# Transposing q and k in two row halves, loading dilated v without overlap, and reordering constants and weights in an attention and gated-unit kernel

## The chip, the cores and the metric

The kernel runs on one core of one Trainium2 chip. The metric is device time in microseconds (us); lower is better. A profiled execution gives a span, from the first to the last instruction, and a time of its own that is a little longer.

## What is computed

Two stages follow each other. The first is sliding-window attention over 8 batches and 8 heads, 576 positions, head size 64; heads 0 to 3 see the last 32 positions ("plain"), heads 4 to 7 every fourth of the last 128 ("dilated"). The second is a gated unit over the 512 joined columns.

```python
pos = np.arange(S)
rel = pos[:, None] - pos[None, :]
mask_plain = (rel >= 0) & (rel < window)
mask_dil = (rel >= 0) & (rel < window * dilation) & (rel % dilation == 0)
...
attn = np.exp(scores)
attn = attn / (np.sum(attn, axis=-1, keepdims=True) + 1e-09)
return np.matmul(attn, v).astype(np.float32)
...
for k in range(K):
    gate_pre += conv_w[k][None, None, :] * xp[:, k:k + S, :]
gate = 1.0 / (1.0 + np.exp(-gate_pre))
val = x @ w_val
return (gate * val @ w_out).astype(np.float32)
```

## The kernel before, in words

The work is cut into 16 units: for each batch one dilated and one plain unit of four heads (dilated first, except in the last batch). A unit has two halves of two heads, called `e`. For each unit q and k are loaded (576 KB each, one transfer on SP's queue), brought to bf16 (the dilated ones by reading the high half of each fp32 value, the plain ones by casts on POOL), transposed on TensorE with an identity (line 469, nine 128x128 transposes per matrix into a pair of PSUM banks), and copied to `qT` and `kT` in SBUF, each matrix in two halves on ACT or DVE (line 323 or 325). Then come scores (line 488), exp (508), masks (514), attention products (525 dilated, 552 plain), norms (535, 564) and transposes back to `xT` (573, 589).

When both units of a batch are done, the gated unit follows for each of four column groups: convolution by diagonal weights (607), tanh (615), val product (622), gate (631), and, per 128 rows, the output product (638), a copy to one of six `osb` buffers (643) and a store (652).

Three tile shapes occur on TensorE: whole array (128*128, called `F`: transposes, dilated attention products, val, outputs), two row halves (64*128, `R`: dilated scores, plain attention products) and four quarters (64*64, `Q`: plain scores, convolution).

The order on every engine is written by a planner (class `Plan`): each task has a key (a priority, in part from the table `KEY`), an assumed duration, the engines that may run it, and dependencies; a greedy list scheduler lays out the whole program and the instructions are issued in that order. [...]Where the planner expects TensorE to idle, it puts in matmuls on a zero tile (`warm`, line 666). Loads and stores share SP's queue; a load waits there until enough of the earlier ones have landed, so that few are in flight.

What the change touches:

- `load_q` (422), `load_vd` (434): loads. Dilated v is loaded in two overlapping pieces per unit: `va0` holds 80 keys, `va1` 112 more behind 16 rows of zeros (`Z1`), since the second block of 72 queries needs keys that the first piece already brought. `cv` (787) casts them to `vd0` and `vd1` on POOL.
- `transposes` (461), `evict_t` (474): the transposes of q and k and their way out of PSUM.
- `scores`, `attn_d`, `norm_d`, `transpose_xd`: the blocks of queries, `QB = 72` twice.
- the constants (`band` to `dve_consts`, 328 to 396): identities, masks and zeros, most of them on POOL, and `diag` (673), the diagonal weights, on POOL.
- `WV = 0` and `WO = 1` in `KEY`: w_val is loaded behind the loads of unit 0, w_out behind those of unit 1.

The dependencies of the transposes and of the casts:

```python
TQ[u] = add(f"T{name}{u}", j0 + KEY["T"], {"PE": (0.50, 0.67)},
            lambda t, u=u, name=name: transposes(t, u, name),
            [L[u] if d else C[u], c_eye], cfg="F", need="pair", mm=JP)
...
cvv[(u, e, z)] = add(f"cv{i}{z}", 2 * i + KEY["cv"], {"POOL": (0.57, 0.63)}, cv,
                     [ldv[u][z]] + dep, port=("POOL",))
```

Of the kernel before, what the change touches and what calls it, by code (L numbers as in the profile page):

```python
# [1 line left out]

# [11 lines left out]
def hi_bf16(ap: bass.AP) -> bass.AP:  # L14
# [5 lines left out]
KEY = {"L": 171.6, "cv": -104.8, "T": -8.3, "ET": -139.2, "S": -21.7, "X": -137.2, "M": -69.8, "A": -31.3,  # L20
       "N": -35.2, "XT": 3.1, "XE": -124.1, "C": -15.3, "H": -46.4, "V": -4.0, "G": -205.2, "O":
       33.0, "P": -86.6, "SP": 2, "W": 10.4, "WV": 0, "WO": 1}
# [19 lines left out]
class Plan:  # L42
# [50 lines left out]
    def start_of(self, t, eng):  # L93
        s = self.free_at[eng]
        if eng == "PE" and t.cfg != self.cfg and self.cfg is not None:
            s += self.SWITCH
# [132 lines left out]
def kernel(  # L229
# [10 lines left out]
    nc = tc.nc  # L240
# [8 lines left out]
    QB = TT // 2  # L249
    KB = (80, 128)  # L250
    T1 = TT - KB[1]
    Z1 = 16
# [9 lines left out]
    ETW = 400  # L262
# [25 lines left out]
    xnd = [consts.tile([QB, 8, 2, D], BF16, name=f"xnd{i}") for i in range(2)]  # L288
# [8 lines left out]
    ident_f = consts.tile([8, 8], FP32, name="ident_f")  # L297
    mask_d = consts.tile([128, HALF], BF16, name="mask_d")
# [29 lines left out]
    def band(dst, base, pattern, step):  # L328
        nc.gpsimd.affine_select(out=dst, in_=dst, compare_op=ALU.is_ge, fill=0.0,
                                base=base, pattern=pattern, channel_multiplier=-step)  # L330
        nc.gpsimd.affine_select(out=dst, in_=dst, compare_op=ALU.is_ge, fill=0.0,
                                base=W - 1 - base, pattern=[[-a, n] for a, n in pattern],
                                channel_multiplier=step)

    def eye(dst, n):
        nc.gpsimd.memset(dst, 0.0)
        nc.gpsimd.affine_select(
            out=dst, in_=dst, compare_op=ALU.not_equal, fill=1.0,
            base=0, pattern=[[-1, n]], channel_multiplier=1)

    def const(name, eng, dur, emit, deps=(), key=-50):
        return plan.add(name, key, {eng: (dur, dur + 0.05)}, lambda t: emit(), deps,
                        port=("POOL",))

    c_warm = const("warm0", "DVE", 0.5, lambda: nc.vector.memset(warm, 0.0), key=-60)  # L345
    c_eye = const("eye", "POOL", 1.0, lambda: eye(ident_b, 128), key=-60)
# [4 lines left out]
    c_sw = const("swap", "DVE", 0.25, swapped_eye, deps=[c_eye], key=5)  # L351

    def dil_mask():
        nc.gpsimd.memset(mask_d, 1.0)
        for z in range(2):
            band(mask_d[:, 2 * QB * z:2 * QB * (z + 1)].rearrange("p (h t) -> p h t", h=2),
                 z * (QB - T1), [[0, 2], [1, QB]], 1)

    c_md = const("mask_d", "POOL", 1.6, dil_mask, key=-57)

    def dil_ones():
        for x in vds[0] + vds[1] + vpb:
            nc.gpsimd.memset(x[:, :, :, D:DA], 1.0)
    c_vd = const("ones_d", "POOL", 0.4, dil_ones, key=-56)

    def small_eyes():
        eye(ident_f, 8)
        eye(ident_2[0:64], D)
        nc.gpsimd.tensor_copy(ident_2[64:128], ident_2[0:64])
    c_id = const("eyes", "POOL", 0.9, small_eyes, key=-55)  # L370

    def plain_mask():
        nc.gpsimd.memset(mask_p, 1.0)
        for s in range(2):
            m = mask_p[0:64, s, 0:96]
            nc.gpsimd.affine_select(out=m, in_=m, compare_op=ALU.is_ge, fill=0.0,
                                    base=W - s, pattern=[[1, 96]], channel_multiplier=-2)
            nc.gpsimd.affine_select(out=m, in_=m, compare_op=ALU.is_ge, fill=0.0,
                                    base=s - 1, pattern=[[-1, 96]], channel_multiplier=2)
        for g in range(1, NG):  # L380
            nc.gpsimd.tensor_copy(mask_p[0:64, :, 96 * g:96 * g + 96], mask_p[0:64, :, 0:96])
        nc.gpsimd.tensor_copy(mask_p[64:128], mask_p[0:64])
        nc.gpsimd.memset(mask_p[0:W // 2, :, 0:96], 0.0)
    c_mp = const("mask_p", "POOL", 2.6, plain_mask, key=-10)

    def dve_consts():
        for x in kTs:
            nc.vector.memset(x[:, 0:W], 0.0)
            nc.vector.memset(x[:, W + 2 * S:], 0.0)
        for x in ets:  # L390
            nc.vector.memset(x[:, :, HALF:], 1.0)
        nc.vector.memset(xT[:, :, :, 0:K - 1], 0.0)
        nc.vector.memset(vps[0][0:W // 2, 0], 0.0)
        for x in vas[1]:
            nc.vector.memset(x[0:Z1], 0.0)
    c_dv = const("dve_consts", "DVE", 2.2, dve_consts, key=-59)
# [25 lines left out]
    def load_q(u, name):  # L422
# [4 lines left out]
        if d:  # L427
            return [nc.sync.dma_start(
                out=dst, in_=src[b, hs].rearrange("h (p j) d -> (h p) (j d)", j=JD))]
# [4 lines left out]
    def load_vd(u, n, z):  # L434
        b = units[u][0]
        rows = v[b, 4:8].rearrange("h (p r) d -> p h (r d)", r=R)
        if z == 0:
            return [nc.sync.dma_start(out=vas[z][n % 2], in_=rows[0:KB[0]])]
        return [nc.sync.dma_start(out=vas[z][n % 2][Z1:KB[1]], in_=rows[T1 + Z1:TT])]

# [20 lines left out]
    def transposes(t, u, name):  # L461
        d = units[u][1]
        if d:
            src = (qns if name == "q" else kns)[u % NQ]
        else:
            src = (qcs if name == "q" else kcs)[(u // 2) % 2]
        ps = pair(t).bitcast(BF16)
        for j in range(JP):
            nc.tensor.transpose(  # L469
                out=ps[:, j * 128:(j + 1) * 128],  # L470
                in_=hi_bf16(src)[:, j * 128:(j + 1) * 128] if d else flat(src[:, j]),
                identity=ident_b)

    def evict_t(t, tr, u, name, half):
        dst = kTs[u % 2][:, W:W + 2 * S] if name == "k" else qTs[u % 2]
        pv = pair(tr).bitcast(BF16)[:, 0:JP * 128].rearrange("p (j a) -> p a j", j=JP)
        dv = dst.rearrange("p (a j) -> p a j", j=JP)
        a = slice(64 * half, 64 * half + 64)
        copy(t, dv[:, a], pv[:, a])

    def scores(t, i, hf):
# [10 lines left out]
        if units[u][1]:  # L492
            for z in range(2):
                for hh in range(2):
                    o = (2 * e + hh) * 2 * TT + hf
                    for x in range(2):
                        mm(0, 128, (2 * z + hh) * QB, QB, x, W + o + 2 * z * T1, 2,
                           o + 2 * z * QB, 2)
# [18 lines left out]
    def attn_d(t, sc, i, hf):  # L517
# [3 lines left out]
        for z in range(2):  # L521
            for x in range(2):
                for hh in range(2):
                    c = 2 * z + hh
                    nc.tensor.matmul(out=ps[:, x * 512 + c * DA:x * 512 + (c + 1) * DA],  # L525
                                     lhsT=et[0:KB[z], x, c * QB:c * QB + 128],
# [3 lines left out]
    def norm_d(t, sc, i, hf):  # L530
        av = pair(sc).rearrange("p (x c) -> p x c", x=2)[0:QB, :, 0:4 * DA].rearrange(
            "p x (n c) -> p x n c", n=4)
        rec = work.tile([QB, 2, 4], FP32, name="rec", bufs=3)
# [4 lines left out]
            in0=av[:, :, :, 0:D], in1=rec[:, :, :, None].to_broadcast([QB, 2, 4, D]),  # L538
# [29 lines left out]
    def transpose_xd(t, i):  # L568
        xn = xnd[i % 2]
        pv = bank(t).bitcast(BF16)[:, 0:S].rearrange("p (r t) -> p r t", r=R)  # L570
        for r in range(R):
            for z in range(2):
                nc.tensor.transpose(out=pv[:, r, QB * z:QB * z + QB],  # L573
                                    in_=flat(xn[:, 2 * r + z]),
                                    identity=ident_b[0:QB, 0:QB])
# [81 lines left out]
    def conv_tr(t):  # L657
# [15 lines left out]
    T_DG = add("diag", 4, {"POOL": (2.4, 2.5)}, lambda t: nc.gpsimd.tensor_tensor(  # L673
        out=diag, in0=ident_2[:, None, :].to_broadcast([128, NCH * K, D]),
        in1=conv_w[:, :, None].to_broadcast([128, NCH * K, D]), op=ALU.mult),
        [T_CE, c_id], port=("POOL",))
# [249 lines left out]
```

## Time and profile before

| what | us |
|---|---|
| median of three runs | 186.14 |
| lowest and highest run | 184.7 and 188.52 |
| the profiled execution, its own time | 189.71 |
| its span | 188.0 |
| mean granted TensorE clock | 0.984 |

The profile names an instruction by line, engine, operation, output and input. Its groups of instructions give the busy time, the mean duration of one, and the idle time of the engine just before. Some of the groups that the change touches (busy us, mean ns after the bar's left side; then idle us and what ended it):

```profile
L323 ACT COPY qT<-ps 128x576 bf16<-128x576 bf16 x26 | 15.7, 642 | 6.4 <-PE ps L469 5.6
L325 POOL CAST vd<-va 80x512 bf16<-80x512 f32 (+1 forms) x32 | 19.3, 632 | 44.8 <-DMA va<-in_v_dram 35.3
L666 PE MATMUL ps<-warm 128*128 128x512 bf16 x52 | 15.1, 415 | 2.4 <-DVE warm L345 1.3
```

The loads, with size and median us from issue to landing:

```profile
qn<-in_q_dram SPq DMA_DIRECT2D x16, 576.0 KB, 5.4
kn<-in_k_dram SPq DMA_DIRECT2D x16, 576.0 KB, 6.9
...
va<-in_v_dram SPq DMA_DIRECT2D x8, 448.0 KB, 7.8
va<-in_v_dram SPq DMA_DIRECT2D x8, 320.0 KB, 7.0
```

Matmuls overlap, so that the duration of one is not its price: the distance between the starts of two neighbours is. An engine that sits idle costs nothing unless something on the way to the end waits for it.

### The profile page before, as it was taken

How to read it: one execution, taken by the hardware profiler on the slowest of the kernel's cores; microseconds unless marked ns; L12 is line 12 of the kernel's file. 1: busy time of each engine (PE TensorE's matmuls, PEld its weight loads, DVE VectorE, ACT ScalarE, POOL GpSimd, SP SyncE). 2: the span in 40 equal slices, each digit the busy share in tenths (PEclk: the TensorE clock that was granted, in tenths of full speed). 3: DMA queues.
4: the chain of work that ended last, by engine and by line, in shares of the span. 5: the costliest groups of instructions: out<-in, count | busy, mean ns of one | idle time of the engine just before them, and what ended most of it. 6: DMA issues, size and time to landing. Idle time of an engine off the chain costs nothing.

```text
span 188.0 us, 6710 instructions
## 1 busy us (share of the span) xinstructions
PE 165.5 (88%) x2872; PEld 112.4 (60%) x2896; DVE 120.7 (64%) x233; ACT 124.3 (66%) x210; POOL 62.5 (33%) x99
## 2 busy tenths in 40 slices
PE   7988898998998999987998999789998999989930
PEld 2535455775685667664676677647676567557410
DVE  7498484795688858872877677567785488605000
ACT  2446799568775958684587846988777766672260
POOL 7974307325430723035153540711543230000000
PEclk9999999999999999996999999999999999999997
DMA  5999999899989988996799999859987840143265
GB/s 196 281 391 233 388 267 283 237 265 273 255 232 323 293 193 241 240 279 163 204 318 267 275 308 245 194 190 231 348 202 234 231 167 3 59 152 127 67 210 170
DMA packets 32102, 43.41 MB, mean 231 GB/s; under 512 B 1877, under 2 KB 20293, under 8 KB 32074
## 3 DMA queue, kind: packets, MB, share of 16 engines
q1 hardware_dynamic: 32064, 42.99, 80.7%
q8 instruction: 22, 0.36, 0.9%
q14 instruction: 6, 0.05, 0.1%
q10 hardware_dynamic: 10, 0.01, 0.0%
HBM read 33.56 MB, written 9.44 MB: 229 GB/s over the span
## 4 chain that ended last, share of the span: by engine, by line
PE 54%; DVE 12%; DMA 11%; ACT 11%; issue 6%; SPq 1%; ACTq 1%
PE ps L622 14%; PE ps L638 12%; PE ps L607 8%; PE ps L488 5%; PE ps L469 5%; DMA va<-in_v_dram 4%; ACT et L508 3%; DMA kn<-in_k_dram 3%; DVE et L514 3%; ACT osb L643 3%; DMA wst<-in_moe_w_out_dram 3%; PE ps L552 3%; PE ps L525 3%; DVE xnd L535 2%; PE ps L573 2%
## 5 line engine op out<-in xcount | busy, mean ns | idle before, releaser
L508 ACT ACTIVATE et<-ps 128x576 bf16<-128x576 f32 x64 | 40.6, 654 | 15.8 <-PE ps L488 14.6
L638 PE MATMUL ps<-w_out,gy 128*128 128x512 bf16 x125 | 34.0, 384 | 3.7 <-ACT osb L643 1.5
L622 PE MATMUL ps<-xT,w_val 128*128 128x288 bf16 x256 | 36.1, 287 | 0.6 <-DVE et L514 0.2
L325 POOL CAST vd<-va 80x512 bf16<-80x512 f32 (+1 forms) x32 | 19.3, 632 | 44.8 <-DMA va<-in_v_dram 35.3
L643 ACT ACTIVATE osb<-ps 128x512 f32<-128x512 f32 x36 | 20.8, 604 | 17.4 <-PE ps L638 11.4
L631 DVE SCALAR_TENSOR_TENSOR gy<-gy,ps 128x576 bf16<-128x576 bf16 x32 | 24.0, 750 | 12.6 <-PE ps L622 12.3
L622 PEld LDWEIGHTS <-w_val 128*128 128x128 bf16 x256 | 23.5, 97 | 8.3 <-issue 1.6
L607 PE MATMUL ps<-xT,diag 64*64 64x288 bf16 x640 | 24.6, 286 | 2.7 <-issue 1.8
L514 DVE TENSOR_TENSOR et<-et,mask_d 128x576 bf16<-128x576 bf16 x32 | 20.3, 640 | 8.7 <-ACT et L508 8.5
L615 ACT ACTIVATE gy<-ps 128x576 bf16<-128x576 f32 x32 | 20.4, 657 | 5.1 <-PE ps L607 4.6
L535 DVE TENSOR_TENSOR xnd<-ps,rec 72x512 bf16<-72x512 f32 x32 | 22.0, 687 | 1.1
L638 PEld LDWEIGHTS <-gy 128*128 128x128 bf16 x144 | 13.1, 99 | 15.5 <-issue 4.4
L325 POOL CAST vpb<-vp 128x768 bf16<-128x768 f32 x16 | 14.5, 935 | 22.3 <-DMA vp<-in_v_dram 18.2
L607 PEld LDWEIGHTS <-diag 64*64 64x64 bf16 x640 | 17.1, 106 | 6.7 <-issue 4.6
L488 PE MATMUL ps<-qT,kT 64*64 64x96 bf16 (+1 forms) x640 | 18.5, 205 | 1.8 <-ACT kT L323 1.1
L323 ACT COPY qT<-ps 128x576 bf16<-128x576 bf16 x26 | 15.7, 642 | 6.4 <-PE ps L469 5.6
L514 DVE TENSOR_TENSOR et<-et,mask_p 128x576 bf16<-128x576 bf16 x32 | 15.3, 493 | 6.0 <-ACT et L508 5.6
L488 PEld LDWEIGHTS <-kT 64*64 64x64 bf16 (+1 forms) x640 | 11.5, 102 | 12.8 <-issue 9.0
L323 ACT COPY kT<-ps 128x576 bf16<-128x576 bf16 x24 | 14.6, 646 | 4.1 <-PE ps L469 2.1
L666 PE MATMUL ps<-warm 128*128 128x512 bf16 x52 | 15.1, 415 | 2.4 <-DVE warm L345 1.3
L325 POOL CAST kc<-kn 128x1152 bf16<-128x1152 f32 x8 | 10.7, 1340 | 15.7 <-DMA kn<-in_k_dram 15.7
L323 ACT COPY xT<-ps 128x576 bf16<-128x576 bf16 (+1 forms) x19 | 13.6, 723 | 3.2 <-PE ps L638 2.0
(67 smaller groups left out, 179.2 us busy)
## 6 DMA issues: line engine op xcount, KB each, us to landing
qn<-in_q_dram SPq DMA_DIRECT2D x16, 576.0 KB, 5.4
kn<-in_k_dram SPq DMA_DIRECT2D x16, 576.0 KB, 6.9
out_dram<-osb SPq DMA_DIRECT2D x24, 256.0 KB, 3.2
vp<-in_v_dram SPq DMA_DIRECT2D x15, 384.0 KB, 6.0
va<-in_v_dram SPq DMA_DIRECT2D x8, 448.0 KB, 7.8
va<-in_v_dram SPq DMA_DIRECT2D x8, 320.0 KB, 7.0
out_dram<-osb SPq DMA_DIRECT2D x8, 192.0 KB, 2.3
wst<-in_moe_w_val_dram SPq DMA_DIRECT2D x2, 512.0 KB, 5.9
```

The source lines that it names most:

```text
L323: nc.scalar.copy(out=dst, in_=src)
L325: op(t.eng).tensor_copy(dst, src)
L488: nc.tensor.matmul(out=ps[po:po + pn, x, out_c:out_c + ln], lhsT=kw[rb, k0:k0 + (pn - 1) * kstep + 1:kstep], rhs=qT[rb, q0:q0 + (ln - 1) * ...
L508: nc.scalar.activation(out=ets[(2 * i + hf) % NE][:, :, 0:HALF], in_=ps[:, :, 0:HALF], func=AF.Exp, scale=scale)
L514: op(t.eng).tensor_tensor(out=ev, in0=ev, in1=m.to_broadcast([128, 2, HALF]), op=ALU.mult)
L535: nc.vector.tensor_tensor(out=xnd[i % 2][:, 4 * hf:4 * hf + 4].rearrange("p (x j) h d -> p x (j h) d", x=2), in0=av[:, :, :, 0:D], in1=rec ...
L607: nc.tensor.matmul(out=ps[o:o + 64, 512 * f:512 * f + HALF], lhsT=diag[lo:lo + 64, c * K + kk, :], rhs=xT[lo:lo + 64, b % NX, c, f * HALF ...
L615: nc.scalar.activation(out=gy[:, c, :, b, :], in_=ps[:, :, 0:HALF], func=AF.Tanh, scale=0.5)
L622: nc.tensor.matmul(out=ps[:, 512 * f:512 * f + HALF], lhsT=w_val[f][:, mc, c * 128:(c + 1) * 128], rhs=xT[:, b % NX, mc, K - 1 + f * HALF: ...
L631: nc.vector.scalar_tensor_tensor(out=y, in0=y, scalar=1.0, in1=ps[:, :, 0:HALF], op0=ALU.add, op1=ALU.mult)
L638: nc.tensor.matmul(out=ps, lhsT=y[:, c, 128 * n:128 * n + 128], rhs=w_out[f][:, c, :], start=(c == 0), stop=(c == NCH - 1))
L643: nc.scalar.activation(out=osb[z % NO], in_=bank(ou), func=AF.Copy, scale=0.5)
```

## The change

1. Each transpose of q and k becomes two of 64 partitions: rows 0 to 63 go to one PSUM bank and rows 64 to 127 to the bank beside it, as 64*128 tiles (`R`). A matrix takes 18 transposes of 64 columns instead of nine of 128. For unit 0 the two halves are tasks of their own, each behind a load of 64 partitions of its own, and the scores of unit 0 need only the halves of their two heads.
2. Dilated v: the blocks of queries become 80 and 64 (`QB`), the keys 96 and 128 (`KB`), of which the first 16 of the first block are zeros. Each row is loaded once: 80 rows (320 KB) and 64 rows (256 KB). The 32 keys that the second block shares with the first are cast from `va0` to `vd1` in an extra copy, which the planner may put on POOL, ACT or DVE; 13 of the 16 are on POOL, two on DVE, one on ACT. Rows 0 to 31 of `vd1` are zeroed once.
3. Constants: one band of 128x128 is made on POOL and copied to `mask_d` on DVE; the plain mask is made once for two positions and copied on DVE; identities are copied on DVE; `diag` is multiplied on DVE. POOL zeroes rows of `va0`, `vd1` and `vp0`.
4. `WV = 1`, `WO = 2`: w_val is loaded behind the loads of unit 1, w_out behind those of unit 2. The first loads on SP are now q, k (first halves), q, k (second halves), va0, va1, q and k of unit 1, vp of unit 1, w_val, q and k of unit 2, va of unit 2, w_out, q and k of unit 3.
5. All other keys of the table have new values, outputs have one more (`OB`), and the planner's price of leaving shape `Q` grows by 0.035. By these the order of all engines is another: TensorE's list has 6,338 instructions instead of 5,790, 42 of them filler matmuls instead of 56, and 140 changes of tile shape instead of 147. Behind the last val product stand seven output tiles instead of eight. Three of the 36 output copies are on DVE.

The diff, cut to its core:

```diff
-KEY = {"L": 171.6, "cv": -104.8, ... "SP": 2, "W": 10.4, "WV": 0, "WO": 1}
+KEY = {"L": 124.0, "cv": -169.4, ... "SP": 2, "W": 13.3, "WV": 1, "WO": 2, "OB": 6.3}
...
-            s += self.SWITCH
+            s += self.SWITCH + (0.035 if self.cfg == "Q" else 0.0)
...
-    QB = TT // 2
-    KB = (80, 128)
-    T1 = TT - KB[1]
-    Z1 = 16
+    QB = (80, 64)
+    KB = (96, 128)
+    T0 = (-16, 16)
...
-    ETW = 400
+    ETW = 352
...
+    c_bd = const("band", "POOL", 0.7, bands, [c_one], key=-59)
+
+    def dil_mask():
+        for z in range(2):
+            o = z * QB[0] - T0[z]
+            nc.vector.tensor_copy(
+                mask_d[:, col(z, 0):col(z, 2)].rearrange("p (h t) -> p h t", h=2),
+                band[:, None, o:o + QB[z]].to_broadcast([128, 2, QB[z]]))
+        nc.vector.memset(mask_d[0:-T0[0], 0:col(0, 2)], 0.0)
+    c_md = const("mask_d", "DVE", 0.5, dil_mask, [c_bd], key=-57)
...
+    def rows():
+        for x in vas[0]:
+            nc.gpsimd.memset(x[0:-T0[0]], 0.0)
+        for x in vds[1]:
+            nc.gpsimd.memset(x[0:32], 0.0)
+        nc.gpsimd.memset(vps[0][0:W // 2, 0], 0.0)
+    c_va = const("rows", "POOL", 2.0, rows, key=-55)
...
         if d:
+            rows = slice(0, 128) if part is None else slice(64 * part, 64 * part + 64)
             return [nc.sync.dma_start(
-                out=dst, in_=src[b, hs].rearrange("h (p j) d -> (h p) (j d)", j=JD))]
+                out=dst[rows],
+                in_=src[b, hs].rearrange("h (p j) d -> (h p) (j d)", j=JD)[rows])]
...
-        if z == 0:
-            return [nc.sync.dma_start(out=vas[z][n % 2], in_=rows[0:KB[0]])]
-        return [nc.sync.dma_start(out=vas[z][n % 2][Z1:KB[1]], in_=rows[T1 + Z1:TT])]
+        o = QB[0] * z
+        return [nc.sync.dma_start(out=vas[z][n % 2][o - T0[z]:o - T0[z] + QB[z]],
+                                  in_=rows[o:o + QB[z]])]
...
         for j in range(JP):
-            nc.tensor.transpose(
-                out=ps[:, j * 128:(j + 1) * 128],
-                in_=hi_bf16(src)[:, j * 128:(j + 1) * 128] if d else flat(src[:, j]),
-                identity=ident_b)
+            for n, h in enumerate(parts):
+                a = slice(64 * h, 64 * h + 64)
+                o = 512 * ((t.slot[0] + n) % 2)
+                ps = PS[t.slot[0] // 2][:, o:o + 512].bitcast(BF16)
+                nc.tensor.transpose(out=ps[:, j * 64:(j + 1) * 64],
+                                    in_=src[a, j * 128:(j + 1) * 128], identity=ident_b[a, a])
...
-    T_DG = add("diag", 4, {"POOL": (2.4, 2.5)}, lambda t: nc.gpsimd.tensor_tensor(
+    T_DG = add("diag", 4, {"DVE": (1.40, 1.45)}, lambda t: nc.vector.tensor_tensor(
...
-            TQ[u] = add(f"T{name}{u}", j0 + KEY["T"], {"PE": (0.50, 0.67)},
-                        lambda t, u=u, name=name: transposes(t, u, name),
-                        [L[u] if d else C[u], c_eye], cfg="F", need="pair", mm=JP)
+            if u == 0:
+                TQ[u] = [add(f"T{name}{u}{h}", j0 + KEY["T"], {"PE": (0.36, 0.53)},
+                             lambda t, name=name, h=h: transposes(t, 0, name, (h,)),
+                             [L[u][h], c_eye], cfg="R", need="bank", mm=JP) for h in range(2)]
+            else:
+                TQ[u] = [add(f"T{name}{u}", j0 + KEY["T"], {"PE": (0.31, 0.48)},
+                             lambda t, u=u, name=name: transposes(t, u, name),
+                             (L[u] if d else [C[u]]) + [c_eye], cfg="R", need="pair", mm=2 * JP)]
...
+                for z, to, a, p in ((0, 0, slice(0, KB[0]), slice(0, KB[0])),
+                                    (0, 1, slice(64, 96), slice(32, 64)),
+                                    (1, 1, slice(64, 128), slice(64, 128))):
+                    cvv.setdefault((u, z), []).append(add(
+                        f"cv{i}{z}{to}", 2 * i + KEY["cv"],
+                        {"POOL": (0.57, 0.63), "ACT": (0.52, 0.62), "DVE": (0.35, 0.42)}
+                        if u == 0 or to > z else {"POOL": (0.57, 0.63)},
+                        partial(cv, z=z, to=to, a=a, p=p), [ldv[u][z]] + dep, port=("POOL",)))
...
-                                 lambda t, i=i, h=h: scores(t, i, h), Eq[u] + Ek[u],
+                                 lambda t, i=i, h=h: scores(t, i, h),
+                                 [Eq[u][e], Ek[u][e]] if u == 0 else Eq[u] + Ek[u],
...
-            key = 8 * b1 + 7 + KEY["O"] + (z % 4)
+            key = 8 * b1 + 7 + KEY["O"] + KEY["OB"] * (b1 - 4) + (z % 4)
```

## The prediction

> **What bounds the kernel now.** I read the busy totals first, then the span cut in three (fill, middle, drain), then TensorE's rows one by one.
>
> ```profile
> PE 165.5 (88%) x2872; PEld 112.4 (60%) x2896; DVE 120.7 (64%) x233; ACT 124.3 (66%) x210; POOL 62.5 (33%) x99
> ...
> PE 54%; DVE 12%; DMA 11%; ACT 11%; issue 6%; SPq 1%; ACTq 1%
> ```
>
> ```profile
> 0.00:30.00 30.00, 25.76 (x355) 14.50 (x361) 20.96 (x46) 18.62 (x30) 16.36 (x46) 1.00 0.99 293
> 30.00:173.00 143.00, 132.34 (x2484) 94.59 (x2502) 98.70 (x186) 101.47 (x173) 46.16 (x54) 0.99 0.82 227
> 173.00:188.00 15.00, 7.36 (x36) 3.29 (x34) 1.07 (x2) 4.24 (x8) 0.00 (x0) 0.91 0.46 140
> ```
>
> The columns are the stretch, its length, busy us of PE, PEld, DVE, ACT and POOL, granted clock, DMA share, GB/s. In the fill the DMA engines are full (0.99), and PE's busy time is mostly filler: L666 holds 15.1 us of the run, all before 32 us. In the middle PE is busy 93% of the time, DVE and ACT 70%, DMA 82%: PE bounds it. In the drain nothing is full; the chain of waits runs there through output copies and stores. PE's own rows in the middle give the prices:
>
> ```profile
> 135.17 1.15 PE L622 MATMUL ps<-xT,w_val 128*128 128x288 bf16 x8
> 136.26 0.45 PE L488 MATMUL ps<-qT,kT 64*64 64x96 bf16 x24
> 136.64 1.16 PE L622 MATMUL ps<-xT,w_val 128*128 128x288 bf16 x8
> 137.63 0.42 PE L573 MATMUL ps<-ident_b,xnd 72*128 72x72 bf16 x8
> ...
> 140.79 0.67 PE L469 MATMUL ps<-ident_b,qc 128*128 128x128 bf16 x9
> 141.39 0.55 PE L552 MATMUL ps<-vpb,et 64*128 64x65 bf16 x24
> 141.86 0.81 PE L607 MATMUL ps<-xT,diag 64*64 64x288 bf16 x20
> ```
>
> Read start to start. Eight val matmuls hold PE 0.99 us when the next task has the same array shape (136.64 to 137.63) and 1.09 when it changes (135.17 to 136.26): a **change of shape costs 0.10**. Nine transposes take (0.67 - 0.22)/8 = 56 ns apiece (0.22 is one alone), 0.51 us a matrix. The row-half matmuls of L552, (0.55 - 0.19)/23, and of L488's 64*128 form, (0.44 - 0.20)/15 (its x16 row at 155.92), take **16 ns apiece**.
>
> The profiled execution took 189.71 us, 188.0 of span and 1.7 around it; the median of the runs is 186.14. The gap has a place:
>
> ```profile
> 83.81 1.78 issue
> ```
>
> ```profile
> 87.00:88.00 1.00, 1.00 (x10) 0.50 0.50 151
> ```
>
> PE stands 1.78 us with nothing shown to wait for (chain), and then the granted clock is at half speed for about 3.4 us, 86.3 to 89.7 (one-us stretches): 1.8 + 1.7 = 3.5 us lost. 189.71 - 3.5 = 186.2, the median; so the sum below starts from 186.1.
>
> [...]16 ns against 56, and 0.10 us a change. [...]the trace has 96 ns for 64 rows and 98 for 128, so 18 half loads are not each half price, but in L552 the loads keep up with 16 ns. [...]The trace's only 64-partition loads (vp, 15 to 17.5 us)[...]:
>
> ```profile
> 11.00:14.00 3.00, 2.36 (x25) 1.00 1.06 392
> 14.00:15.00 1.00, 1.00 (x12) 1.00 1.14 292
> 15.00:17.50 2.50, 1.86 (x42) 1.00 1.23 216
> ```
>
> [...]one mask took 3471 ns while POOL ran diag and four casts (9.3 to 13.1 us), where 452 is the median.
>
> **The change part by part.**
>
> *Transposes.* Per matrix nine at 56 ns become 18 at 16: 0.51 to 0.29, -0.22 us. Units 2 to 15 hold 28 matrices, on PE's path: -6.2. Those of units 0 and 1 lie in the fill, behind loads: 0. The new form has another shape than before, so shape changes count: the instruction order has 147 before and 140 after, -7 x 0.10 = -0.7. PE is 93% busy in the middle, so some of the 6.9 comes back as waits on evictions: I take 85%, **-5.9** (ends: -3, half lost, and -7). Evictions move as many elements as before (0.65 us on ACT, 0.75 on DVE): 0.
>
> *Fill.* Prices from rates: a q+k pair, 1.18 MB at 392 GB/s, 3.0 us; a weight pair, 1.05 MB, 2.7; a vp pair, 0.79 MB at 216, 3.6; va before 0.79 MB at 240 (6.5 to 9 us), 3.3; va after 0.59 MB, 2.5; the first q+k at 350, 3.4. To unit 2's k the order before is 3.4 + 3.3 + 2.7 + 3.0 + 3.6 + 2.7 + 3.0 = 21.7; after, with w_val behind unit 1 and w_out behind unit 2, 3.4 + x + 2.5 + 3.0 + 3.6 + 2.7 + 3.0 = 18.2 + x. x is the price of loading unit 0's q and k as four 64-partition transfers[...]; I take 1.0. Two more issues on SP, 0.45 us each, are inside x. So k2 comes 2.5 earlier, and k3, with w_out now ahead of it, 3.5 - (2.7 - 0.8) - 1.0 = 0.6 earlier. Before, T of k2 starts at 27.10 and T of k3 at 36.49, k3 landed at 34.12 and its cast ended at 35.3. After, PE gets there at 24.6 + 9.4 - 0.4 (two shorter T) + 0.8 (the swap matmuls, now in this stretch) = 34.4, the cast at 34.7: gain 36.5 - 34.7 = **-1.8**[...].
>
> *Constants.* POOL loses masks and diag and gets zeroing: 0.5 (identity) + 2 x 0.91 (va, at DVE's price) + 3 x 0.53 (vd, from 0.58 for 576 columns) + 0.2, then the bands, until about 6.0. DVE's mask copies wait for these, and behind them in its order stand diag (about 1.3, 1280 columns), the eviction of k and the first masks; the first attention product waits for those. That is about 8.5, against a first mask at 9.34 and a diag ending at 10.3 before. What hides any delay is unit 1's k, landed near 13: cover 3 us, cost 0.
>
> *v.* 16 copies of 32 partitions are added, 13 on POOL at about 0.61 = 7.9 us; POOL waits 35 us for va in the run, so 0.[...] The middle's loads fall from 6.0 + 3.3 + 3.6 + 3.0 (stores) = 15.9 us of DMA per batch to 15.1, against a PE period of (121.2 - 43.7 - 3.5)/4 = 18.5 (T of k, units 4 to 12) that becomes 17.5. Norms and the d-transposes keep their columns: 0.
>
> *Instruction supply.* PE's list grows by 548. Queue 8 brought 22 packets, 0.36 MB, for 5,790 instructions; that makes two more. Cost +0.3; ends 0 and +3.5, one more stall such as the one above.
>
> *Drain.* After the last val matmul eight output tiles become seven (the order lists), and one pair of buffers is filled before the last four val tasks.
>
> ```profile
> 178.93 0.60 ACT L643 ACTIVATE osb<-ps 128x512 f32<-128x512 f32 x1 [2.58 <-DMA out_dram<-osb]
> 180.20 2.56 ACT L643 ACTIVATE osb<-ps 128x512 f32<-128x512 f32 x5 [0.68 <-DMA out_dram<-osb]
> ```
>
> The copies wait 3.3 us for a buffer, and the last ends at 182.76, 2.35 after PE's last product at 180.41. The next wait is on the second use of the other buffer: I take **-1.0** (ends 0, -2.4).
>
> Sum: -5.9 - 1.8 + 0.3 - 1.0 = -8.4, so 186.1 - 8.4 = 177.7, said as **178**.
>
> **Rivals.** (a) *Loads arrive no sooner than PE asked before.* For it: T of k waits for its load at 27.10 and 81.15 (0.15 us each), and the casts of k wait 15.7 us in 8 times for landings; a faster PE walks into them. Against: PE's waits on DMA are 0.3 us in all, the share in the middle is 0.82. Then -3 + 0.3 - 0.2 and no gain in the drain: 183.2.
> (b) *Slower: the two halves don't run side by side.* Then 18 x 56 ns = 1.0 us a matrix, +0.5 x 28 = +14, with the other terms -2.5: 197.6. It decides from 41 ns apiece: (189.9 - 186.1 + 2.5)/28 + 0.51 = 0.73 us a matrix. Against: L552 and L488 at 16 ns with the same row halves. That they are transposes no row shows.
> (c) *The change doesn't do what it says*: not so, the order lists show 576 half transposes, the smaller va loads and the moved weights.
>
> **How the numbers follow.** Forecast 0.77, its own range 174.5 to 181.5; (a) 0.15; (b) 0.05; something else on the slow side 0.03. 2% of 186.1 is 3.7 us, about what a measurement tells from no change: faster below 182.4. The forecast and a little of (a): 0.78; the rest of (a): 0.14; (b) and other: 0.08. The range 174 to 184 holds the forecast's and (a).
>
> **What would show it.** Half transposes at 16 ns start to start, about 0.3 us a matrix; the period of T of k at 17.5; T of k2 near 24.6 and of k3 near 34.7; the last copy within 1.5 us of PE's last product. Wrong: first loads landing over 2 us later (x), T rows at 40 ns or more, PE waiting on DMA for more than 2 us after 35, or DVE or ACT over 80% in the middle.

## The result and the profile after

The changed kernel took 204.77 us (median of four runs, 203.95 to 205.8), the kernel before beside it 187.33 us (184.7 to 190.17): a ratio of 1.105, 95% interval 1.093 to 1.116. The prediction said 178 us. Slower by about 17 us where it said faster by 8.

The busy totals of the kernel after, and its chain of waits by engine:

```profile
PE 172.5 (85%) x3145; PEld 115.5 (57%) x3170; DVE 130.2 (64%) x262; ACT 121.1 (60%) x204; POOL 67.1 (33%) x92
...
PE 58%; DVE 16%; ACT 10%; DMA 7%; issue 5%; SPq 1%; ACTq 0%; DVEq 0%
PE ps L646 14%; PE ps L662 12%; PE ps L598 7%; PE ps L631 7%; DVE et L538 5%; PE ps L512 4%; PE ps L690 4%; DMA kn<-in_k_dram 3%; ACT osb L667 3%; PE ps L549 3%; DVE gy L655 2%; PE ps L492 2%; PE ps L613 2%; ACT et L532 2%; DVE xnp L588 2%
```

TensorE's busy time grew by 7 us, although the transposes got shorter. The chain shows a line that the prediction priced at nothing: L598, the transposes back to `xT` of the dilated half, with 7% of 203.5 us. The groups of instructions with each shape apart (busy us and mean ns behind the bar, then idle us before):

```profile
L598 PE MATMUL ps<-ident_b,xnd 80*128 80x80 bf16 x64 | 13.5, 211 | 1.5 <-ACT qT L324 0.9 <-ACT kT L324 0.4
L598 PE MATMUL ps<-ident_b,xnd 64*128 64x64 bf16 x64 | 12.9, 202 | 0.0
```

The same line before (L573, all of 72 rows):

```profile
L573 PE MATMUL ps<-ident_b,xnd 72*128 72x72 bf16 x128 | 6.5, 198 | 0.5 <-ACT xT L323 0.5
```

The mean of one is about 200 ns in all three. The two groups lie over each other in time, so their busy times can't be added; the page's line for both together says 18.8 us, against 6.5 before:

```profile
L598 PE MATMUL ps<-ident_b,xnd 80*128 80x80 bf16 (+1 forms) x128 | 18.8, 206 | 1.5 <-ACT qT L324 0.9
```

The column that tells is the tile: 80*128 and 64*128 by turns. Rows of TensorE in the middle of the kernel after (start, us, instruction):

```profile
137.12 0.44 PE L492 MATMUL ps<-ident_b,qn 64*128 64x64 bf16 x18
137.38 0.55 PE L576 MATMUL ps<-vpb,et 64*128 64x65 bf16 x24
137.75 0.44 PE L492 MATMUL ps<-ident_b,kn 64*128 64x64 bf16 x18
...
146.27 1.15 PE L598 MATMUL ps<-ident_b,xnd 80*128 80x80 bf16 x8
```

Eighteen half transposes take 0.44 us, 14 to 16 ns apiece: that price was right. But eight transposes back take 1.15 us where the task took 0.42 before. The span cut as before (columns as in the prediction):

```profile
0.00:30.00 30.00, 21.59 (x271) 12.24 (x274) 19.44 (x59) 11.73 (x19) 14.33 (x27) 0.74 0.95 237
30.00:188.50 158.50, 143.06 (x2843) 99.44 (x2857) 108.71 (x201) 105.59 (x178) 52.81 (x66) 0.98 0.74 208
188.50:203.50 15.00, 7.81 (x41) 3.81 (x39) 2.06 (x3) 3.75 (x7) 0.00 (x0) 0.96 0.41 126
```

In the fill TensorE did 271 instructions instead of 355, at a granted clock of 0.74. T (the task of the transposes) of unit 2's k starts at 33.0 us (27.1 before), of unit 3's k at 44.7 (36.5). The rows of unit 2's k, before and after:

```profile
27.10 0.68 PE L469 MATMUL ps<-ident_b,kn 128*128 128x128 bf16 x9
```

```profile
32.96 0.44 PE L492 MATMUL ps<-ident_b,kn 64*128 64x64 bf16 x18
```

The chain's first 20 us show a part of the reason:

```profile
2.71 6.10 DMA kn<-in_k_dram
8.81 0.05 issue
8.86 1.21 PE ps L492 x9
...
10.98 5.00 PE ps L690 x14
15.98 0.26 PE ps L549 x8
```

The second half of k lands at 8.81 us; then 14 fillers (L690), which stand in order ahead of the first attention product (L549), take 5.0 us, most of it at half clock (7.9 to 14.7 us). Before, 15 fillers took 3.63 us there. The clock is at half once more from 21.5 to 31.8 us.

Later there is a stall of the kind seen before, now inside a row of half transposes (chain of waits):

```profile
52.77 0.20 PE ps L492 x13
52.97 1.75 issue
54.72 0.26 PE ps L492 x5
```

The clock is at 0.5 afterwards, 55.6 to 59.1 us.

### The profile page after: what moved, and what is told of

Same layout as the page of the kernel before. It is cut to its first block, busy times and chain, and to the rows that moved or that the text cites. A ratio compares the mean times of both kernels' runs of the same rounds, so it can differ in the third digit from the quotient of the medians.

```text
span 203.5 us, 7277 instructions
## 1 busy us (share of the span) xinstructions
PE 172.5 (85%) x3145; PEld 115.5 (57%) x3170; DVE 130.2 (64%) x262; ACT 121.1 (60%) x204; POOL 67.1 (33%) x92
## 4 chain that ended last, share of the span: by engine, by line
PE 58%; DVE 16%; ACT 10%; DMA 7%; issue 5%; SPq 1%; ACTq 0%; DVEq 0%
PE ps L646 14%; PE ps L662 12%; PE ps L598 7%; PE ps L631 7%; DVE et L538 5%; PE ps L512 4%; PE ps L690 4%; DMA kn<-in_k_dram 3%; ACT osb L667 3%; PE ps L549 3%; DVE gy L655 2%; PE ps L492 2%; PE ps L613 2%; ACT et L532 2%; DVE xnp L588 2%
## 5 line engine op out<-in xcount | busy, mean ns | idle before, releaser
L326 POOL CAST vd<-va 64x512 bf16<-64x512 f32 (+2 forms) x44 | 29.4, 674 | 59.7 <-DMA va<-in_v_dram 58.0
L655 DVE SCALAR_TENSOR_TENSOR gy<-gy,ps 128x576 bf16<-128x576 bf16 x32 | 24.0, 751 | 18.9 <-PE ps L646 15.4
L667 ACT ACTIVATE osb<-ps 128x512 f32<-128x512 f32 x33 | 18.5, 599 | 21.4 <-PE ps L662 14.3
L631 PE MATMUL ps<-xT,diag 64*64 64x288 bf16 x640 | 26.3, 295 | 2.2 <-ACT xT L324 1.0
L559 DVE TENSOR_TENSOR xnd<-ps,rec 80x512 bf16<-80x512 f32 x32 | 22.0, 687 | 1.1
L326 POOL CAST vpb<-vp 128x768 bf16<-128x768 f32 x16 | 13.9, 895 | 24.5 <-DMA vp<-in_v_dram 18.2
L512 PE MATMUL ps<-qT,kT 64*64 64x96 bf16 (+2 forms) x640 | 18.8, 210 | 2.2 <-ACT kT L324 1.0
L538 DVE TENSOR_TENSOR et<-et,mask_d 128x576 bf16<-128x576 bf16 x32 | 16.7, 540 | 5.7 <-ACT et L532 5.5
L512 PEld LDWEIGHTS <-kT 64*64 64x64 bf16 (+1 forms) x640 | 13.1, 107 | 12.8 <-issue 10.5
L598 PE MATMUL ps<-ident_b,xnd 80*128 80x80 bf16 (+1 forms) x128 | 18.8, 206 | 1.5 <-ACT qT L324 0.9
L538 DVE TENSOR_TENSOR et<-et,mask_p 128x576 bf16<-128x576 bf16 x32 | 18.1, 597 | 2.5 <-ACT et L532 2.5
L324 ACT COPY xT<-ps 128x576 bf16<-128x576 bf16 (+1 forms) x16 | 11.7, 728 | 12.0 <-PE ps L662 8.4
L690 PE MATMUL ps<-warm 128*128 128x512 bf16 x36 | 13.5, 507 | 4.4 <-DVE kT L326 1.5
```

What stands on the lines that cost most here:

```text
L324: nc.scalar.copy(out=dst, in_=src)
L326: op(t.eng).tensor_copy(dst, src)
L512: nc.tensor.matmul(out=ps[po:po + pn, x, out_c:out_c + ln], lhsT=kw[rb, k0:k0 + (pn - 1) * kstep + 1:kstep], rhs=qT[rb, q0:q0 + (ln - 1) * ...
L538: op(t.eng).tensor_tensor(out=ev, in0=ev, in1=m.to_broadcast([128, 2, HALF]), op=ALU.mult)
L559: nc.vector.tensor_tensor(out=xnd[i % 2][:, 4 * hf:4 * hf + 4].rearrange("p (x j) h d -> p x (j h) d", x=2), in0=av[:, :, :, 0:D], in1=rec ...
L598: nc.tensor.transpose(out=pv[:, r, o:o + n], in_=flat(xn[0:n, 2 * r + z]), identity=ident_b[0:n, 0:n])
```

## The experiments

All start from after.py unless "before" is said; each changes only what its diff shows, and the order on the engines stays unless the text says otherwise. The theory after the result: the alternating tiles of L598 cost the time. Its rivals: the other parts of the change (halves, fill, weights) do.

**Transposes back with one tile.** Each reads 80 rows; the 16 extra columns land where the next block overwrites them or are never read.

```diff
+        n = QB[0]
         for r in range(R):
             for z in range(2):
-                o, n = QB[0] * z, QB[z]
-                nc.tensor.transpose(out=pv[:, r, o:o + n], in_=flat(xn[0:n, 2 * r + z]),
+                o = TT * r + QB[0] * z
+                nc.tensor.transpose(out=pv[:, o:o + n], in_=flat(xn[0:n, 2 * r + z]),
                                     identity=ident_b[0:n, 0:n])
```

> The changed kernel with one edit: all transposes back to xT read 80 rows, so that none of them is a 64-row tile between 128-row ones; the order of all engines stays the same. Theory A (TensorE changes tile shape at every transpose of the task that brings dilated attention back, 264 changes in all instead of the 140 that were counted): the task falls from 1.15 to about 0.42 us, 16 times, 11.7 us, of which some comes back as waits: 193 to 196 us. Theory B (the fill is what costs: first loads in halves, a low clock, late weights): the task falls, but the time stays above 200.

191.02 us, ratio to before 1.025 (1.018 to 1.033). All these transposes together are busy 7.3 us, and one task takes 0.45 us again:

```profile
L599 PE MATMUL ps<-ident_b,xnd 80*128 80x80 bf16 x128 | 7.3, 201 | 1.5 <-ACT qT L324 0.9 <-ACT kT L324 0.4
```

```profile
136.19 0.45 PE L599 MATMUL ps<-ident_b,xnd 80*128 80x80 bf16 x8
```

That is some 14 of the 17.4 us, from one detail of one helper. It comes back in three places: T of unit 2's k starts at 28.0 instead of 33.0, from there to T of unit 15's k it takes 130.2 us instead of 136.6, and the rest is 1.8 shorter.

In the middle the price comes out: 12 of the tasks lie between these two marks, 12 x (1.15 - 0.45) = 8.4 us. Less the stalls without a shown reason and what the half clock behind them costs, by an estimate half its length (together 3.5 us after, 5.6 here; in the kernel before twelve transposes of L589 take 0.68 us at a granted clock of 1.00, at 66.4 us, and 1.14 at 0.50, at 88.1), the stretch is 133.1 against 124.6 us, 8.5 shorter. In the fill it does not: only two tasks lie ahead of unit 2's k there, 19.4 and 24.6 us, some 1.7 us of the 5.0. The rest goes with the second stretch at half clock, which this run does not have (its fill is at full clock from 14.8 us on). The mean clock of the four runs says the same, 0.931 to 0.948 after and 0.965 to 0.996 here. How the alternation leads to that half clock is not shown.

**The same, sorted.** Four blocks of 80 rows, then four of 64: one change within a task instead of seven.

```diff
-        for r in range(R):
-            for z in range(2):
+        for z in range(2):
+            for r in range(R):
```

> The changed kernel with the eight transposes of that task sorted: four of 80 rows, then four of 64; 168 changes of shape. Theory A: one change inside the task instead of seven, the task at about 0.55 us, total within 3 us above the run with 80 rows throughout. Theory B: above 200.

192.79 us, ratio 1.035 (1.027 to 1.042), from two runs: near the other, a little slower, as 168 changes against 140 should be (28 at 0.10 us are 2.8). One task:

```profile
137.22 0.52 PE L598 MATMUL ps<-ident_b,xnd 80*128 80x80 bf16 x8
```

With the rows as wide as in the kernel after, only their sequence changed, and the task takes 0.52 us instead of 1.15: so the alternation is the cost, not the 64-row form.

**Half transposes alone, in the kernel before** (line 461 as in the change; order as before, 165 changes of shape instead of 147).

```diff
+            for h in range(2):
+                a = slice(64 * h, 64 * h + 64)
+                ps = PS[t.slot[0] // 2][:, 512 * h:512 * h + 512].bitcast(BF16)
+                nc.tensor.transpose(out=ps[:, j * 64:(j + 1) * 64],
+                                    in_=src[a, j * 128:(j + 1) * 128], identity=ident_b[a, a])
```

> The kernel before with one part of the change alone: q and k transposed in two row halves, 18 transposes of 64 columns a matrix, the order of all engines unchanged; changes of shape 165 instead of 147. The price of the prediction (16 ns apiece, 0.22 us a matrix saved, 0.10 us a change of shape) gives 28 x 0.22 - 18 x 0.10 = 4.4 us less: about 182 to 184. If the halves cost more than they save: 187 or more.

192.28 us, ratio 1.030 (1.023 to 1.037): a miss. What the prediction called its largest gain is a loss when done alone; 18 more changes of shape at 0.10 us are 1.8 of the 6 us. The rows have the price expected (18 in 0.44 us, (0.44 - 0.19)/17 = 15 ns apiece), but the trace, of an execution of 195.04 us, has two stalls of the unexplained kind and, up to 115 us, 10.2 us at half clock (3.4 before). Two of the three stretches at half clock follow these stalls, the first a wait for unit 2's k. The three other runs, of 191.4 to 192.8 us, have a mean clock of 0.968 to 0.971, against 0.986 to 0.994 in seven of the eight runs of the kernel before beside them. The larger stall, in the chain:

```profile
84.06 0.37 PE ps L471 x18
84.44 0.37 PE ps L551 x24
84.80 0.24 PE ps L606 x3
85.05 3.09 issue
88.13 1.89 PE ps L606 x33
```

**Unit 0's q and k in whole loads** (with 80-row transposes back), which tests the 64-partition loads.

```diff
-                out=dst[rows],
-                in_=src[b, hs].rearrange("h (p j) d -> (h p) (j d)", j=JD)[rows])]
+                out=dst, in_=src[b, hs].rearrange("h (p j) d -> (h p) (j d)", j=JD))]
```

> The changed kernel with 80 rows throughout and q and k of unit 0 loaded in one transfer of 128 partitions each, in the places of their first halves; the order stays the same. Theory A: the first loads are hidden, within 1.5 us of the run with 80 rows alone. Theory B: the last of these loads lands 2 us earlier, TensorE doesn't idle and keeps its clock in the fill, and the time falls by 3 to 6 us more.

192.1 us, 188.29 to 194.41 (no ratio, the runs differ too much), not shown to be better than 191.02. T of unit 2's k is at 29.0 instead of 28.0: in this trace the halves of the first loads are not what holds the fill.

**Fillers half as long** (with 80-row transposes back): 256 columns instead of 512.

```diff
-        out=bank(t), lhsT=warm[:, 0:128], rhs=warm, start=True, stop=True)
+        out=bank(t)[:, 0:256], lhsT=warm[:, 0:128], rhs=warm[:, 0:256], start=True, stop=True)
```

> The kernel after with all transposes back reading 80 rows (191.0 us, T of unit 2's k at 28.0, first attention product at 15.74), each filler matmul now 256 columns instead of 512; order and instruction count are the same. Theory: in the fill the first attention product has its masks at 13.04 and its v at 12.73 us, but stands in order behind 14 fillers that run at half clock from 10.7 to 15.9. With half of each, it starts near 13.3, T of unit 2's k comes 1 to 2.5 us earlier, and the time is 188.5 to 190. Rival: the loads of units 1 and 2 set the fill; then the attention product is earlier, T of unit 2's k stays at 28.0 and the time at 191.

The chain of this kernel, at the place of the 5.0 us shown above:

```profile
10.87 3.15 PE ps L691 x14
14.02 0.40 PE ps L549 x8
```

The first attention product starts at 14.02 instead of 15.74, T of unit 2's k at 26.7 instead of 28.0: the fillers do hold a part of the fill. The profiled execution was 189.25 us, but the median of four is 192.41 (189.25 to 196.91): in the time, no gain is shown.

**q and k transposed whole again** (with 80-row transposes back): units 1 to 15 by nine transposes of 128x128.

```diff
+        if len(parts) == 2:
+            ps = pair(t).bitcast(BF16)
+            for j in range(JP):
+                nc.tensor.transpose(out=ps[:, j * 128:(j + 1) * 128],
+                                    in_=src[:, j * 128:(j + 1) * 128], identity=ident_b)
+            return
```

> The kernel after with all transposes back reading 80 rows (191.0 us), and q and k of units 1 to 15 transposed whole, nine of 128x128, as in the kernel before; order otherwise the same; changes of shape 137 instead of 140, TensorE's list 5,795 instructions instead of 6,335. The prediction's price (0.22 us a matrix on TensorE's path, 28 matrices) says slower by 5 to 6: 196 to 197. Rival: 540 more instructions cost[...] what the halves save; then 189 to 192, with fewer or shorter stalls without a shown reason.

188.85 us, ratio 1.012 (1.007 to 1.017): faster by 2.2 than with halves, where the prediction's price said slower by 5 to 6. There is no stall over 0.4 us without a shown reason. What the halves did to TensorE is read over the same work, from T of unit 2's k to T of unit 15's k, first with halves (the kernel of the first experiment), then whole:

```profile
28.00:158.20 130.20, 116.10 (x2546) 81.50 (x2545) 97.25 (x180) 92.20 (x157) 51.19 (x66) 0.99 0.84 237
```

```profile
27.90:154.90 127.00, 119.56 (x2313) 86.14 (x2312) 97.82 (x179) 92.33 (x157) 53.40 (x66) 1.00 0.88 245
```

With halves TensorE is busy 3.5 us less (3.4 us at half clock lengthen its busy time there, by that estimate by 1.7) and idle 14.1 us instead of 7.4, 6.7 more. Of its waits from 30 to 170 us with halves, 3.9 us have no shown reason, 5.0 are for ACT and 4.5 for DVE; whole they are 0, 3.9 and 3.2.

**The stalls.** Counting weight loads ahead of each (two instructions to a load: 6,338 and 3,170 in the kernel after, 5,790 and 2,896 before) gives a pattern:

```
kernel                       stall at us   loads ahead   instructions   beyond a multiple of 256
before                       83.81         1371          2742           182
after                        52.97         733           1466           186
80 rows                      46.86         733           1466           186
80 rows                      106.30        1881          3762           178
halves in before             85.05         1499          2998           182
halves in before             107.13        1882          3764           180
```

All stand about 180 beyond a multiple of 256, and in each case the 256 instructions before had gone in 3.8 to 5.2 us, where 7 is usual (80 rows, 30 to 170 us: 2,687 loads in 140 us, 6.7 us for 128). The other runs with the list of the 80-row kernel (sorted, whole loads, shorter fillers) stall behind 733 loads too, for 1.6 to 2.3 us. Not every such place stalls: one at 3.9 us (88 us, 80 rows) did not, nor did the place behind 1,881 loads in the sorted run. The author's estimate, from these places and from the packets on the two pages: instructions come to TensorE some 256 at a time, and a stall comes where 256 were used up fast. The instruction queue (q8) brought 25 packets, 0.41 MB, for the 6,338 instructions after, 254 to a packet, and 22, 0.36 MB, for the 5,790 before, 263 to a packet. The planner of both kernels reckons with blocks too, but of 125 matmuls (`LINE = 125`), where the stalls stand whole multiples of 128 weight loads apart, or nearly. To test the estimate, the list was shifted.

**Each filler of the kernel before in two**, of 256 columns; the same filler time, 112 instructions more.

```diff
+    plan.idle = lambda t: [nc.tensor.matmul(
+        out=bank(t)[:, 256 * n:256 * n + 256], lhsT=warm[:, 0:128], rhs=warm[:, 0:256],
+        start=True, stop=True) for n in range(2)]
```

> The kernel before with each filler of 512 columns as two of 256: the same work, 112 instructions more on TensorE, nearly all ahead of 32 us. Theory (instruction supply): stalls stand at fixed places of the instruction list, 180 beyond a multiple of 256; the stall at 83.8 us with 1,371 weight loads before it either stays at 1,371 loads and so falls 1 to 4 us earlier, or goes, or comes at another such place; the time is 183.5 without a stall, 187 with one, 190 with two. Rival (the stall belongs to the work being done): it comes again at 83.8 us, behind 1,427 loads, and the time is 187.

The longest stall left is 0.53 us, which speaks against the rival; the theory, as put down, allowed for any other outcome. The time did not follow: 190.49 us, ratio 1.021 (1.017 to 1.024), with a later fill (T of unit 2's k at 29.7 instead of 27.1, half clock from 17.8 to 21.2 us). TensorE waits there for unit 1's q, whose cast starts at 15.7 us instead of 13.8; why it comes later is not shown. From there to T of unit 15's k it is shorter than before, 124.4 against 126.3 us.

**Weights behind units 1 and 2, in the kernel before** (a new order follows).

```diff
-... "WV": 0, "WO": 1}
+... "WV": 1, "WO": 2}
```

> The kernel before with w_val loaded behind unit 1 and w_out behind unit 2, as in the kernel after, and the planner's order that follows; all else as before (changes of shape 142 instead of 147, 62 fillers instead of 56). The prediction's arithmetic of loads says one weight pair less ahead of unit 2, 2.7 us: T of unit 2's k from 27.1 to 24.5, of unit 3's k about the same, so that the time gains 0 to 1.5 (185.5 to 187). Rival: the serial work of unit 0 and 1 sets the fill; T of unit 2's k stays within 1 us of 27.1, w_val's casts fall into the work of unit 1, and the time is 187 to 190.

195.44 us (192.08 to 196.84; no ratio, the runs differ too much). T of unit 2's k at 26.2, 0.9 earlier, not 2.7. In the new order 17 output tiles stand behind the last val product instead of eight (rows of TensorE in this kernel's drain):

```profile
164.83 2.61 PE L622 MATMUL ps<-xT,w_val 128*128 128x288 bf16 x20
167.28 14.84 PE L638 MATMUL ps<-w_out,gy 128*128 128x512 bf16 x68
```

With the old keys the planner lets the outputs pile up; it says little of the weights alone, and that part stays open.

**Fillers in four and in three**, 80-row transposes back, halves kept. Four (of 128 columns) adds 252 instructions, three (of 170, written alike) 168, all ahead of 41 us.

```diff
-        out=bank(t), lhsT=warm[:, 0:128], rhs=warm, start=True, stop=True)
+        out=bank(t)[:, 128 * n:128 * n + 128], lhsT=warm[:, 0:128], rhs=warm[:, 0:128],
+        start=True, stop=True) for n in range(4)]
```

> The kernel after with all transposes back reading 80 rows (191.0 us), each filler of 512 columns as four of 128: the same filler time, six instructions more on TensorE for each, some 170 more by 45 us and 252 in all; the work and its order are the same. Theory (instruction supply): the stalls at 46.86 us (behind 733 weight loads) and 106.3 us (behind 1,881) stand at fixed places of the list, which now hold other work. By the run with whole fillers, the 256 instructions before the new places take 5.7 us or more nearly everywhere, against 3.9 us ahead of the stall at 46.86. So both stalls go or fall under 1 us, no stretch at half clock follows, and the time is 186 to 188.5. Rival (dense transposes stall by themselves): stalls of 1.5 us or more inside the transposes of q and k near 47 and 106 us again, time 190 to 192.

The stall near 106 us went, the one near 47 stayed, so as a test of the two theories it was ill chosen: 252 is nearly one block. The chain, whole fillers first, then fillers in four:

```profile
46.66 0.20 PE ps L492 x13
46.86 2.16 issue
49.02 0.34 PE ps L492 x5
```

```profile
47.49 0.27 PE ps L492 x15
47.76 2.59 issue
50.35 0.23 PE ps L492 x3
```

It moved by two transposes, which are four instructions, and 256 - 252 is four; 861 loads stand ahead of it, 186 instructions beyond a multiple of 256. No half clock follows this stall of 2.6 us. 190.6 us, ratio 1.019 (1.012 to 1.027).

> The kernel after with all transposes back reading 80 rows (191.0 us), each of the 42 fillers as three of 170 columns: 168 instructions more on TensorE, all ahead of 40 us; work and order the same. (Fillers in four added 252, one block of 256 less four, so that nearly the same work stood at the blocks' ends; the stall near 47 us moved by two transposes, four instructions.) Theory (instruction supply, ends of blocks at 180 beyond a multiple of 256): the ends now stand 168 instructions earlier in the work, where the 256 before took 5.7 and 5.8 us by the run with whole fillers. No stall over 1 us near 47 or 106 us; the quickest blocks are now one ending near 30 us (4.8 us) and one near 155 (4.3), where one may come. Time 187.5 to 189.5. Rival (the transposes stall by themselves): stalls over 1.5 us inside the transposes of units 4 and 10 near 47 and 106 us; time 190 to 192.

The same stretch, fillers in three (chain):

```profile
46.65 0.47 PE ps L576 x24
47.12 0.26 PE ps L492 x18
47.38 0.02 issue
47.40 1.14 PE ps L647 x8
```

Eighteen transposes without a stall, and no stall over 1 us without a shown reason in the run; the longest is 0.8. So the place of these stalls goes with the place in the list, not with the transposes; that it is the supply of instructions that fails there is not shown. The profiled execution took 188.54 us, as expected; but six runs lie between 187.4 and 192.21, median 190.51, with no clear ratio. That a stall-free list makes the kernel faster on the whole was not shown.

**Nine output buffers in the kernel before**, no order changed.

```diff
-    osb = [outbuf.tile([128, Dm], FP32, name=f"osb{i}") for i in range(NO)]
+    osb = [outbuf.tile([128, Dm], FP32, name=f"osb{i}") for i in range(9)]
```

> The kernel before with nine output buffers instead of six, every engine's order unchanged. The prediction's drain says that the last copies stand 3.3 us for a buffer; with nine they stand for nothing but TensorE's last products, and the last copy ends 0.5 to 1 us behind the last product instead of 2.35. Theory: 1 to 2.4 us faster, 183.5 to 185.5 against 186.5. Rival: the stores themselves drain at their own pace and the end moves by less than 0.7.

Ratio 0.991 (0.987 to 0.995), about 1.7 us faster than before, and the fastest kernel of the study (by the medians of all runs, 186.15 against 187.46 us, it is 1.3). The copies now follow their products (rows of ACT in the drain of an execution of 189.04 us):

```profile
177.51 1.08 ACT L643 ACTIVATE osb<-ps 128x512 f32<-128x512 f32 x2 [0.64 <-PE ps L638]
179.24 1.08 ACT L643 ACTIVATE osb<-ps 128x512 f32<-128x512 f32 x2 [0.64 <-PE ps L638]
180.97 1.09 ACT L643 ACTIVATE osb<-ps 128x512 f32<-128x512 f32 x2 [0.64 <-PE ps L638]
```

The wait for `out_dram` that the prediction quoted is gone, and the last copy ends 1.12 us behind the last product instead of 2.35. As order and count are those of the kernel before, so is the stall: 1.59 us, after 37 of the 40 convolution matmuls of L607, where the kernel before stood after 37 as well. A second one, of 1.39 us at 29.2 us, stands behind 350 loads, 188 instructions beyond a multiple of 256; the trace of the kernel before has none there. The 256 instructions ahead of it had gone in about 7.2 us, which is not fast. So the list fixes where a stall can come, not whether it comes.

**The best of after:** 80-row transposes back, whole q and k, fillers of 256 columns, nine output buffers.

> The kernel after with all transposes back reading 80 rows, q and k of units 1 to 15 transposed whole (188.85 us so far), fillers of 256 columns, nine output buffers. From the parts: 188.85, less 1.0 to 1.5 in the fill (T of unit 2's k from 27.9 to 26.6), less 0 to 1 in the drain: 186.4 to 187.9, that is even with the kernel before. Rival: less filler[...] nothing is gained: 189.

Ratio 1.000 (0.997 to 1.004): even with the kernel before. T of unit 2's k starts at 25.5, 1.6 earlier than before; the rest gives it back.

## Why the prediction was wrong, step by step

**Shape changes: the step that failed.** The prediction said "the instruction order has 147 before and 140 after" and took -0.7 us; for the new blocks it said "Norms and the d-transposes keep their columns: 0". Both counted the shape by the kind of task. By the tile that each instruction has, the kernel after has 264 changes: 124 more, seven inside each of the 16 tasks and 12 at their edges. At its own price of 0.10 us that is +12.4; measured by the tasks it is 16 x (1.15 - 0.42) = 11.7, by the run without them 13.8. That these agree so well is in part luck: the 13.8 hold some 3 us of half clock in the fill beyond the two tasks there, and against them the run without the alternation has a stall more. The prediction charged its measured 0.10 us a change for the q and k transposes and did not ask which tile a block of 64 rows gets. The profile of the kernel after prints it: 64*128 beside 80*128.

**Half transposes: price right, worth wrong.** 14 to 16 ns apiece, as worked out. The term that failed is "some of the 6.9 comes back as waits ... I take 85%": with the halves undone the kernel was 2.2 us faster. The freed time became idle time, in part as stalls without a shown reason (3.9 us with halves, none whole) and the half clock behind one of them, in part as waits for DVE and ACT (9.5 us against 7.1). In the run without stalls (fillers in three), T of unit 2's k to that of unit 15's takes 125.7 us against 127.0 with whole transposes, so about 1.3 us of the 6 is left, from one trace of each: TensorE is busy 113.7 us of it against 119.6 (17 matmul records are missing in the first), 5.8 less, and idle 4.5 more. The period of T of k, units 4 to 12, for which 17.5 us was forecast, is 18.9 in that run and 21.3 in the kernel after. The stretch with fillers in three, to be read beside the two under "q and k transposed whole again":

```profile
28.40:154.10 125.70, 113.72 (x2550) 82.11 (x2567) 95.95 (x180) 92.56 (x157) 52.67 (x68) 1.00 0.88 247
```

**Instruction supply.** Taken as +0.3 with an end at +3.5. In the run with 80 rows the stalls are 3.9 us and 3.4 us at half clock, behind one of the two, lose 1.7 more by the estimate above: 5.6, beyond the end. The half clock behind a stall lasts 3.4 us each time; it follows some stalls of 1.4 to 3.1 us, and others of that length (one of 2.6 us) it does not follow.

**Fill.** -1.8 was taken, T of unit 3's k at 34.7; it came at 44.7, and at 39.6 without the alternation. The arithmetic added up loads, while TensorE's order held it: 5.0 us of fillers, most at half clock, ahead of a product whose v and masks were ready (at 12.7 and 13.0 us in the 80-row run, the product at 15.7). Shorter fillers brought T of unit 2's k, forecast at 24.6, from 28.0 to 26.7; what holds the other 2.1 us is not shown. Undoing the half loads showed no gain; x, taken as 1.0, and the -0.2 of rival (a) were the author's estimates, shown by no trace. Moving w_out also brought a wait: SP stands 5.9 us for w_val's casts before it can load w_out into the same buffers, and unit 3's q, behind it, is issued at 30.2 instead of 24.5 us (80 rows: 27.4).

**Constants and v at nothing.** No run isolates them. All that is left when alternation and halves are undone is 1.2% (0.7 to 1.7), about 2 us, and this holds the fill, the weights and the new order as well.

**Drain: right in size.** -1.0 was taken. From the end of the last val product to the end of the last output copy it is 8.4 us against 9.3. The tile less did not shorten TensorE's part, 6.9 us in both, as TensorE now stands 0.7 us for an output copy; the gain is in the copies, whose last ends 1.47 us behind the last product instead of 2.35. The nine buffers confirm that the wait for a buffer cost time there.

**Rivals.** (b) named slower, through halves that do not run side by side; they take 14 to 16 ns apiece, far from the 41 at which (b) begins. The slower side had another mechanism, a change of shape within a task, that no rival named. (a), loads no sooner, was nearer in the fill but names the wrong thing: as far as is shown, it was the order of TensorE and its clock.

## What to carry to other kernels

Count changes of tile shape instruction by instruction, from the tile that the profile prints, and do so for every block whose size a change touches: blocks of 80 and 64 rows by turns cost 0.10 us each time here (1.15 us a task), and with 80 rows for both a task took 0.45 us, where 72 rows had taken 0.42. Splitting matmuls to save array time also spends instructions, and busy time saved on a 93% busy engine may come back whole as waits (here 3.5 us less busy, 6.7 more idle); undo the part alone before counting it. In a fill that an order written ahead holds, look for filler ahead of the first real product (5.0 us here) before adding up loads.

## What was not expected of the hardware

- Transposes of 64 and 80 rows by turns take (1.15 - 0.2)/7 = 0.136 us from start to start, of 80 rows alone (0.45 - 0.2)/7 = 0.036: the change costs 0.10 us also within one task.
- TensorE stalls of 1.1 to 3.1 us without a shown reason stand 178 to 188 beyond a multiple of 256 in its list of instructions, and shifting the list by 168 removes them (0.8 at most), by 252 moves one by four instructions.
- Behind eight of these fourteen stalls the granted clock is 0.5 for 3.4 us, from at most 1.2 us after the stall's end; behind six (one of them 2.6 us long) it stays full.
